# Loading q by single tokens in 256-byte rows, and spacing the attention work of a block's two groups

## The chip, the cores and the metric

The kernel runs on one core of a Trainium2 chip. The metric is the device time of one execution in microseconds (us), lower is better. A core has a matrix engine (TensorE, PE in the profile; its weight loads are listed as PEld), a vector engine (VectorE, DVE), a scalar engine (ScalarE, ACT), a general engine (GpSimd, POOL) and a sync engine (SyncE, SP) that only issues DMAs here. They run side by side and wait for each other by semaphores. 16 DMA engines move data between the chip's memory (HBM) and the on-chip SBUF; TensorE writes its sums to PSUM.

## The reference

Attention in chunks of 64 tokens, then a feed-forward network with a squared ReLU:

```python
B, H, S, D = (8, 8, 576, 64)               # q, k, v, float32
q_c = q.reshape(B, H, 9, 64, D)            # k_c, v_c likewise
scores = 1 / sqrt(D) * q_c @ k_c^T
attn = exp(scores - max) / sum             # along a row of 64
out = attn @ v_c
x = out.transpose(0, 2, 1, 3).reshape(B * S, H * D)     # 4608 x 512
result = max(x @ w_in, 0) ** 2 @ w_out     # w_in 512 x 2048, w_out 2048 x 512
```

## The kernel before

**Tiling.** The 4608 tokens are cut into 18 groups of 256 (a sequence of 576 tokens ends inside some groups), and two groups make a block of the feed-forward network: 9 blocks (the second one takes groups 3 and 2). While block j goes through the network, the groups of block j + 1 go through attention, and q, k and v of block j + 2 are loaded.

**One group's attention** is a chain of steps, each a function:

- `qk_pieces` and `v_pieces` yield the loads, each a DMA that SP issues. Groups 0 to 3 load q and k by pairs of tokens. From group 4 on (`FIRST_DMA_T`), q is loaded by pairs of tokens, in rows of 512 bytes (L103), and k by single tokens, in rows of 256 bytes (L111), a DMA for each 128 tokens or part of them. q and k have five buffers.
- `cast_qk` (C in the plan) makes bfloat16 copies `qkb` of q (L218) and k (L221): on GpSimd for groups 4 to 7, on ScalarE from group 8.
- `transpose_qk_dma` (TD) has one DMA transpose both into `qkT` (L227), issued by SP. The groups before 4 are transposed by TensorE instead (L165).
- `scores` (SC) runs 32 matmuls of 64 x 64 x 64 (L249) into one PSUM tile `ps_att`, of which there are two, and ScalarE takes the exponential (L256). As q lies in pairs, the queries of 64 tokens are two runs of 32 columns, read alternately: the helper `queries` gives this view, in which neighbouring columns are 1,024 bytes apart.
- `values` (AV) runs 64 matmuls in two halves (L273), each half into a `ps_att` tile, and VectorE divides by the row sum (L280, L281).
- `transpose_x` (XT) transposes the result into `xT`: on TensorE with a copy for groups 2 to 5 (L300, L305), with a DMA that SP issues from group 6 on (L294).

**The feed-forward work** is a generator that yields after each unit; a unit is a *slot*. `ffn_in` has a slot for each of 16 column tiles of `w_in` (32 in block 1, which works in halves of 256 tokens): four matmuls (L336), the ReLU on ScalarE (L347) and the square on VectorE (L351) or ScalarE (L349). `ffn_out` computes a 2 x 2 product with seven quarter products instead of eight, in 14 slots of eight matmuls each (L404), with copies on ScalarE (L439, L448, L475), sums on VectorE (L364) and stores of the output that GpSimd issues (L423). Block 0 uses a plain second layer (L485).

**The order of the work** is written out by hand. After each slot, the loop issues one piece of the pending loads, if the slot is in `go_slots`, and then the steps that `plan` has for that slot. Each engine and SP's queue run their instructions in this order. So a transpose on SP stands behind all loads of earlier slots, and scores on TensorE stand in front of all feed-forward matmuls of later slots. The slot tables are at L557 to L592: in block 2, for instance, scores of the next block's groups are at slots 8 and 11, values at 12 and 14, xT at 15 and 17.

Of the kernel before, what the change touches and what calls it, by code (L numbers as in the profile page):

```python
# [17 lines left out]
def kernel(  # L18
# [9 lines left out]
    nc = tc.nc  # L28

    B, H, S, D = q.shape  # L30
# [7 lines left out]
    GT = 256  # L38
# [3 lines left out]
    FIRST_DMA_T = 4  # L42
# [33 lines left out]
    def segments(g0, n):  # L76
        while n:
            b, s = divmod(g0, S)
            m = min(n, S - s)
            yield b, s, m  # L80
            g0 += m
            n -= m

    qk = {}

    def runs(g):

        for t in range(GT // 128):
            p = 0
            for b, s, m in segments(g * GT + t * 128, 128):  # L90
                yield t, p, m, b, s
                p += m

    def qk_pieces(g):
        q_sb = in_pool.tile([128, 2, H, D], FP32, name="q_sb")
        k_sb = in_pool.tile([128, 2, H, D], FP32, name="k_sb")
        qk[g] = (q_sb, k_sb)

        pairs = ((q_sb, q), (k_sb, k)) if g < FIRST_DMA_T else ((q_sb, q),)
        p = 0  # L100
        for b, s, m in segments(g * GT, GT):
            for dst, src in pairs:
                yield lambda dst=dst, src=src, b=b, s=s, p=p, m=m: nc.sync.dma_start(  # L103
                    out=dst.rearrange("p t h d -> p (t h d)")[p:p + m // 2, :].rearrange(
                        "p (h e) -> p h e", h=H),
                    in_=src[b, :, s:s + m, :].rearrange("h (s i) d -> s h (i d)", i=2))
            p += m // 2
        if g < FIRST_DMA_T:
            return
        for t, p, m, b, s in runs(g):  # L110
            yield lambda b=b, s=s, t=t, p=p, m=m: nc.sync.dma_start(  # L111
                out=k_sb[p:p + m, t, :, :],
                in_=k[b, :, s:s + m, :].rearrange("h s d -> s h d"))

    def v_pieces(g):

# [96 lines left out]
    def cast_qk(g):  # L213
        qkb = att_pool.tile([128, 2, 2 * H * D], BF16, name="qkb", bufs=2)
        state["qkb", g] = qkb
        copy = nc.gpsimd.tensor_copy if g < 8 else nc.scalar.copy
        q_sb, k_sb = (x.rearrange("p t h d -> p (t h d)") for x in qk[g])
        copy(  # L218
            out=qkb[:, 0].rearrange("p (i h d) -> p i h d", i=2, h=H),
            in_=q_sb.rearrange("p (h i d) -> p i h d", h=H, i=2))  # L220
        copy(out=qkb[:, 1], in_=k_sb)  # L221

    def transpose_qk_dma(g):
        qkb = state.pop(("qkb", g))
# [5 lines left out]

    def scores(g):
        qkT = state.pop(("qkT", g))

        def queries(a, t, hp, p):
            x = qkT[64 * a:64 * a + 64, 0]
            if g < FIRST_DMA_T:
                return x[:, t, hp, p * 64:p * 64 + 64]
            p0 = (2 * t + p) * 32
            return x[:, :, hp, p0:p0 + 32].rearrange("c i p -> c p i")

        ps = ps_att.tile([128, 1024], FP32, name="ps_att")
        for hp in range(n_hp):
            for t in range(2):
                for a in range(2):
                    for p in range(2):
                        c = p ^ a
                        cols = slice(p * 64, p * 64 + 64)
                        o0 = a * 512 + hp * 128 + t * 64
                        nc.tensor.matmul(  # L249
                            out=ps[64 * c:64 * c + 64, o0:o0 + 64],  # L250
                            lhsT=qkT[64 * a:64 * a + 64, 1, t, hp, cols],
                            rhs=queries(a, t, hp, p),
                            start=True, stop=True)
        e = att_pool.tile([128, 2, n_hp, 2, 64], BF16, name="e")
        state["e", g] = e
        nc.scalar.activation(  # L256
            out=e.rearrange("p a h t q -> p (a h t q)"), in_=ps, func=AF.Exp, scale=scale)
# [48 lines left out]

    C, TD = cast_qk, transpose_qk_dma
    SC, AV, XT = scores, values, transpose_x

    def TA(g):  # L310
# [55 lines left out]
    def sum_quarters(out, in0, in1, op=ALU.add, half=slice(None)):  # L366
        return lambda _: add(nc.vector, out[:, half], in0[:, half], in1[:, half], op)
# [110 lines left out]
    def ffn_out_by_ft(j):  # L478

        gT = gTs.pop(j)  # L480
        n_tt = len(blocks[j]) * GT // 128
        o_ps = [ps_ffn.tile([128, d_model], FP32, name="ps_ffn") for _ in range(n_tt)]

        def mm(tt, ft):
            nc.tensor.matmul(  # L485
                out=o_ps[tt],
                lhsT=gT[:, ft, tt * 128:(tt + 1) * 128],
                rhs=w_out_bf[:, ft, :],
                start=(ft == 0), stop=(ft == n_ft - 1))

        for ft in range(n_ft - 4):
            for tt in range(n_tt):
                mm(tt, ft)
            yield
        for tt in range(n_tt):
            for ft in range(n_ft - 4, n_ft):
                mm(tt, ft)
            o_sb = ffn_pool.tile([128, d_model], FP32, name="o_sb", bufs=4)
            nc.scalar.copy(out=o_sb, in_=o_ps[tt])
            t0 = blocks[j][tt // 2] * GT + tt % 2 * 128  # L500
            nc.gpsimd.dma_start(out=out[t0:t0 + 128, :], in_=o_sb)
# [44 lines left out]
    for j, grps in enumerate(blocks):  # L546
        nxt = blocks[j + 1] if j + 1 < len(blocks) else []
        far = blocks[j + 2] if j + 2 < len(blocks) else []
        plan = {}

        def at(slot, f, g):
            plan.setdefault(slot, []).append((f, g))

        if j == 0:
            loads, go_slots = pieces(far), range(17)
            at(28, sum_quarters(b11_p_b21, b11, b21), None)
            for slot, f in ((24, TA), (27, SC), (29, AV), (31, XT)):  # L557
                at(slot, f, nxt[0])
            at(31, TQ, nxt[1])
            at(31, sum_quarters(b11_m_b22, b11, b22, ALU.subtract), None)  # L560
            phases = [ffn_in(0, [(0, 512, range(n_ft))]), ffn_out_by_ft(0)]
        elif j == 1:
            loads, go_slots = itertools.chain(*map(qk_pieces, far)), range(26, 48)
            for slot, f in ((1, TK), (4, SC), (7, AV), (11, XT)):
                at(slot, f, grps[1])
            for i, g in enumerate(nxt):
                for slot, f in ((16 + 4 * i, C), (21 + 4 * i, TD), (37 + i, SC), (39 + 2 * i, AV),
                                (42 + 2 * i, XT)):
                    at(slot, f, g)
            for i, g in enumerate(far):  # L570
                at(36 + 4 * i, C, g)
                at(42 + 3 * i, TD, g)
            at(2, sum_quarters(b11_p_b12, b11, b12), None)
            at(12, sum_quarters(b12_p_b22, b12, b22), None)
            at(20, sum_quarters(b21_p_b22, b21, b22), None)
            phases = [ffn_in(1, [(0, 256, FT_ORDER), (256, 256, FT_ORDER)]), ffn_out(1)]
        else:
            loads, go_slots = pieces(far), range(32)
            slots = {SC: (4, 4), AV: (7, 10), XT: (11, 13), C: (18, 22), TD: (20, 24)}
            if j == 3:  # L580
                slots.update({SC: (6, 6), AV: (9, 11), XT: (12, 14)})
            if j == 2:
                loads = itertools.chain(*map(v_pieces, nxt), loads)
                slots = {SC: (8, 11), AV: (12, 14), XT: (15, 17), C: (20, 23), TD: (22, 25)}
                go_slots = [*range(18), *range(26, 32)]
            for f in (SC, AV, XT):
                for i, g in enumerate(nxt):
                    at(slots[f][i], f, g)
            for f in (C, TD):
                for i, g in enumerate(far):  # L590
                    at(slots[f][i], f, g)
            phases = [ffn_in(j, [(0, BT, FT_ORDER)]), ffn_out(j)]  # L592
        slot = 0
# [41 lines left out]
```

## Time and profile before

| | |
|---|---|
| median of 7 runs | 291.61 us (290.22 to 296.98) |
| profiled execution | 290.98 us, of it the span from first to last instruction 289.2 us |
| TensorE busy | 274.3 us |
| VectorE, ScalarE, GpSimd busy | 188.3, 161.6, 53.2 us |
| DMA packets | 141,648, of them 110,448 under 512 bytes; 57.09 MB |
| score matmuls (L249) | 576, busy 11.2 us |
| loads of q in 512 KB | 12, median 6.9 us from issue to landing |
| loads of k in 256 KB | 25, median 6.3 us from issue to landing |
| transposes of q and k | 14, median 5.4 us from issue to landing |

The profile is of one execution. Busy time is the time in which an engine has work in it; time in which it stands is put down to what ended it (`[1.01 <-DMA ...]` is a stand of 1.01 us that a DMA ended). The chain of waits goes back from the last instruction: at each step to what released it, or to the instruction before it on its engine. A line such as `L249` is a line of the kernel before. The DMA share is the mean over the 16 DMA engines of the time that their packets took; transfers overlap, so in short stretches it can pass 100%.

### The profile page before, as it was taken

The numbers are of one execution on the slowest core, as the hardware profiler recorded it, in microseconds if no ns is written. First come the engines' busy times: TensorE is split into PE (matmuls) and PEld (weight loads), VectorE is DVE, ScalarE is ACT, GpSimd is POOL, SyncE is SP. The second block draws the span as 40 slices with busy tenths as digits, with TensorE's granted clock in tenths as the row PEclk, the third lists the DMA queues.
The fourth block names the chain that finished last, engine by engine and source line by source line (L and its number), as shares of the span: only waits on it lengthen the run. The fifth ranks groups of instructions, "written<-read, shape, count | busy, mean of one in ns | idle before, by whom it ended". The sixth has DMA issues, their size and how long they took to land.

```text
span 289.2 us, 7266 instructions
## 1 busy us (share of the span) xinstructions
PE 274.3 (95%) x3014; PEld 182.5 (63%) x3014; DVE 188.3 (65%) x305; ACT 161.6 (56%) x270; POOL 53.2 (18%) x85
## 2 busy tenths in 40 slices
PE   2999999989999999989989999999999999999994
PEld 1774455778874488547844785478548844884583
DVE  1256414889854496479637973797389648965793
ACT  1527605776348753866376738763876387308710
POOL 2037744051161003000200021002000200030012
PEclk9999999999999999999999999999999999999999
DMA  7999999999999999998999999978994931121003
GB/s 199 240 332 358 365 320 213 292 222 202 218 181 271 238 194 252 268 224 167 200 257 218 176 198 300 200 134 187 309 214 86 169 124 36 39 99 48 2 18 127
DMA packets 141648, 57.09 MB, mean 197 GB/s; under 512 B 110448, under 2 KB 137328, under 8 KB 141616
## 3 DMA queue, kind: packets, MB, share of 16 engines
q1 hardware_dynamic: 138640, 47.33, 78.6%
q0 software_dynamic: 2832, 9.18, 8.7%
q8 instruction: 23, 0.38, 0.6%
q10 hardware_dynamic: 144, 0.13, 0.1%
q14 instruction: 9, 0.07, 0.1%
HBM read 36.70 MB, written 9.44 MB: 160 GB/s over the span
## 4 chain that ended last, share of the span: by engine, by line
PE 84%; DVE 5%; DMA 5%; ACT 3%; issue 1%; SPq 0%; ACTq 0%
PE ps_ffn L336 37%; PE ps_ffn L404 33%; PE ps_ffn L485 5%; DMA qkT<-qkb 3%; PE ps_att L249 3%; PE ps_att L273 2%; DVE gT L351 2%; ACT rl L347 2%; DMA k_sb<-in_k_dram 2%; PE ps_ffn L211 2%; DVE x L281 2%; PE ps_ffn L165 1%; PE ps_att L300 1%; PE ps_ffn L200 0%; DVE w_out_bf L364 0%
## 5 line engine op out<-in xcount | busy, mean ns | idle before, releaser
L336 PE MATMUL ps_ffn<-xT,w_in_bf 128*128 128x512 bf16 (+1 forms) x640 | 130.1, 358 | 1.1 <-ACT rl L347 0.6
L351 DVE TENSOR_TENSOR gT<-rl 128x512 bf16<-128x512 f32 (+2 forms) x132 | 75.4, 596 | 64.4 <-ACT rl L347 62.9
L347 ACT ACTIVATE rl<-ps_ffn 128x512 f32<-128x512 f32 (+2 forms) x160 | 85.3, 553 | 34.1 <-PE ps_ffn L336 31.5
L336 PEld LDWEIGHTS <-w_in_bf 128*128 128x128 bf16 x640 | 60.6, 98 | 58.7 <-issue 1.3
L404 PEld LDWEIGHTS <-w_st 128*128 128x128 bf16 x640 | 62.3, 98 | 7.6
L423 POOL DMA_DIRECT2D out_dram<-o_sb x29 | 20.8, 717 | 157.7 <-DVE o_sb L364 152.2
L364 DVE TENSOR_TENSOR w_st<-gT 128x2048 bf16<-128x2048 bf16 x40 | 47.4, 1219 | 0.2
L404 PE MATMUL ps_ffn<-w_out_bf,w_st 128*128 128x256 bf16 x384 | 45.0, 273 | 0.0
L404 PE MATMUL ps_ffn<-w_sum,w_st 128*128 128x256 bf16 x256 | 29.6, 273 | 0.0
L404 PEld LDWEIGHTS <-gT 128*128 128x128 bf16 x256 | 25.1, 98 | 4.4
L281 DVE TENSOR_TENSOR x<-ps_att,rec 128x512 bf16<-128x512 f32 x36 | 24.9, 692 | 1.2
L475 ACT COPY o_sb<-ps_ffn 128x512 f32<-128x512 f32 (+1 forms) x8 | 4.5, 560 | 34.7 <-PE ps_ffn L404 34.7
L256 ACT ACTIVATE e<-ps_att 128x1024 bf16<-128x1024 f32 x18 | 17.9, 1020 | 7.7 <-PE ps_att L249 7.5
L349 ACT ACTIVATE gT<-rl 128x512 bf16<-128x512 f32 (+2 forms) x28 | 16.8, 600 | 0.9
L404 PE MATMUL ps_ffn<-w_out_bf,gT 128*128 128x256 bf16 x128 | 15.3, 273 | 0.0
L404 PE MATMUL ps_ffn<-w_sum,gT 128*128 128x256 bf16 x128 | 15.3, 272 | 0.0
L485 PE MATMUL ps_ffn<-w_out_bf,gT 128*128 128x512 bf16 x64 | 14.7, 379 | 0.3 <-ACT rl L347 0.3
L273 PEld LDWEIGHTS <-e 64*64 64x64 bf16 x576 | 7.0, 107 | 9.4 <-DVE x L281 2.7
L249 PEld LDWEIGHTS <-qkT 64*64 64x64 bf16 x576 | 8.8, 109 | 6.2 <-issue 4.0
L249 PE MATMUL ps_att<-qkT 64*64 64x64 bf16 x576 | 11.2, 219 | 1.4 <-DMA qkT<-qkb 1.0
L140 POOL CAST w_in_bf<-w_st 128x1024 bf16<-128x1024 f32 (+1 forms) x9 | 9.0, 1004 | 18.7 <-DMA w_st<-in_moe_w_in_dram 18.6
L273 PE MATMUL ps_att<-ve_sb,e 64*64 64x65 bf16 x288 | 9.9, 197 | 1.9 <-DVE x L281 1.1
(51 smaller groups left out, 161.6 us busy)
## 6 DMA issues: line engine op xcount, KB each, us to landing
out_dram<-o_sb POOLq DMA_DIRECT2D x33, 256.0 KB, 4.7
k_sb<-in_k_dram SPq DMA_DIRECT2D x25, 256.0 KB, 6.3
q_sb<-in_q_dram SPq DMA_DIRECT2D x12, 512.0 KB, 6.9
ve_sb<-in_v_dram SPq DMA_DIRECT2D x32, 128.0 KB, 4.4
vo_sb<-in_v_dram SPq DMA_DIRECT2D x32, 128.0 KB, 3.9
w_st<-in_moe_w_in_dram SPq DMA_DIRECT2D x8, 512.0 KB, 6.7
w_st<-in_moe_w_out_dram SPq DMA_DIRECT2D x8, 512.0 KB, 6.3
k_sb<-in_k_dram SPq DMA_DIRECT2D x3, 512.0 KB, 7.2
```

The lines of the kernel that those rows point to most:

```text
L249: nc.tensor.matmul(out=ps[64 * c:64 * c + 64, o0:o0 + 64], lhsT=qkT[64 * a:64 * a + 64, 1, t, hp, cols], rhs=queries(a, t, hp, p), start=T ...
L256: nc.scalar.activation(out=e.rearrange("p a h t q -> p (a h t q)"), in_=ps, func=AF.Exp, scale=scale)
L273: nc.tensor.matmul(out=ps[64 * p:64 * p + 64, a, hp * (D + 1):(hp + 1) * (D + 1)], lhsT=e[64 * c:64 * c + 64, a, hp, t, :], rhs=vb[64 * c: ...
L281: nc.vector.tensor_tensor(out=x[:, t].rearrange("p h a d -> p a h d"), in0=o[:, :, :, 0:D], in1=rec.to_broadcast([128, 2, n_hp, D]), op=AL ...
L336: nc.tensor.matmul(out=h[:, 0:n], lhsT=w_in_bf[:, dt, ft * 128:(ft + 1) * 128], rhs=xT[:, c // 128:(c + n) // 128, dt, :], start=(dt == 0) ...
L347: nc.scalar.activation(out=rl[:, 0:n], in_=h[:, 0:n], func=AF.Relu)
L349: nc.scalar.activation(out=gT[:, ft, c:c + n], in_=rl[:, 0:n], func=AF.Square)
L351: nc.vector.tensor_tensor(out=gT[:, ft, c:c + n], in0=rl[:, 0:n], in1=rl[:, 0:n], op=ALU.mult)
L364: engine.tensor_tensor(out=out, in0=in0, in1=in1, op=op)
L404: nc.tensor.matmul(out=outs[t], lhsT=a[:, i, t * 128:(t + 1) * 128], rhs=b[:, i, :], start=(first and i == 0 and (last or t == 0)), stop=( ...
L423: dma.dma_start(out=out[t0:t0 + HT, col:col + HD].rearrange("(t p) d -> p t d", p=128), in_=o_sb.rearrange("p (t d) -> p t d", d=HD))
L485: nc.tensor.matmul(out=o_ps[tt], lhsT=gT[:, ft, tt * 128:(tt + 1) * 128], rhs=w_out_bf[:, ft, :], start=(ft == 0), stop=(ft == n_ft - 1))
```

## The change

From group 4 on, q is loaded as k is: by single tokens, in rows of 256 bytes, one DMA for each 128 tokens or part of them, q and k in turn. The cast of q no longer reorders, and the scores read 64 neighbouring columns of `qkT` for every group. SP issues 160 instructions instead of 135.

In the plan, block 1 has scores, values and xT of groups 4 and 5 one slot earlier, and xT of its own second group one slot later. In block 2 the second scores go from slot 11 to 10, the second values from 14 to 15 and the second xT from 17 to 18; in block 3 the second values from 11 to 12 and the second xT from 14 to 15. In the blocks after, scores go from slot 4 to 5, values from 7 and 10 to 8 and 11, the second xT from 13 to 14. Since loads are issued one a slot, and there are two or three more a block, loads of v come later in SP's order, in block 2 partly behind the transposes of q and k.

```diff
     def qk_pieces(g):
...
-        pairs = ((q_sb, q), (k_sb, k)) if g < FIRST_DMA_T else ((q_sb, q),)
...
         for t, p, m, b, s in runs(g):
-            yield lambda b=b, s=s, t=t, p=p, m=m: nc.sync.dma_start(
-                out=k_sb[p:p + m, t, :, :],
-                in_=k[b, :, s:s + m, :].rearrange("h s d -> s h d"))
+            for dst, src in ((q_sb, q), (k_sb, k)):
+                yield lambda dst=dst, src=src, b=b, s=s, t=t, p=p, m=m: nc.sync.dma_start(
+                    out=dst[p:p + m, t, :, :],
+                    in_=src[b, :, s:s + m, :].rearrange("h s d -> s h d"))
...
     def cast_qk(g):
-        copy = nc.gpsimd.tensor_copy if g < 8 else nc.scalar.copy
-        q_sb, k_sb = (x.rearrange("p t h d -> p (t h d)") for x in qk[g])
-        copy(
-            out=qkb[:, 0].rearrange("p (i h d) -> p i h d", i=2, h=H),
-            in_=q_sb.rearrange("p (h i d) -> p i h d", h=H, i=2))
-        copy(out=qkb[:, 1], in_=k_sb)
+        for which in range(2):
+            copy = nc.gpsimd.tensor_copy if g < 8 else nc.scalar.copy
+            copy(out=qkb[:, which], in_=qk[g][which].rearrange("p t h d -> p (t h d)"))
...
     def scores(g):
-        def queries(a, t, hp, p):
-            x = qkT[64 * a:64 * a + 64, 0]
-            if g < FIRST_DMA_T:
-                return x[:, t, hp, p * 64:p * 64 + 64]
-            p0 = (2 * t + p) * 32
-            return x[:, :, hp, p0:p0 + 32].rearrange("c i p -> c p i")
...
-                            rhs=queries(a, t, hp, p),
+                            rhs=qkT[64 * a:64 * a + 64, 0, t, hp, p * 64:p * 64 + 64],
...
-            for slot, f in ((1, TK), (4, SC), (7, AV), (11, XT)):
+            for slot, f in ((1, TK), (4, SC), (7, AV), (12, XT)):
...
-                for slot, f in ((16 + 4 * i, C), (21 + 4 * i, TD), (37 + i, SC), (39 + 2 * i, AV),
-                                (42 + 2 * i, XT)):
+                for slot, f in ((16 + 4 * i, C), (21 + 4 * i, TD), (36 + i, SC), (38 + 2 * i, AV),
+                                (41 + 2 * i, XT)):
...
-            slots = {SC: (4, 4), AV: (7, 10), XT: (11, 13), C: (18, 22), TD: (20, 24)}
+            slots = {SC: (5, 5), AV: (8, 11), XT: (11, 14), C: (18, 22), TD: (20, 24)}
             if j == 3:
-                slots.update({SC: (6, 6), AV: (9, 11), XT: (12, 14)})
+                slots.update({SC: (6, 6), AV: (9, 12), XT: (12, 15)})
             if j == 2:
-                slots = {SC: (8, 11), AV: (12, 14), XT: (15, 17), C: (20, 23), TD: (22, 25)}
+                slots = {SC: (8, 10), AV: (12, 15), XT: (15, 18), C: (20, 23), TD: (22, 25)}
```

More of the change, by code (lines that the diff above doesn't have):

```diff
@@ L97, in qk_pieces @@
         qk[g] = (q_sb, k_sb)
-        pairs = ((q_sb, q), (k_sb, k)) if g < FIRST_DMA_T else ((q_sb, q),)
[L100 to L107, printed above, removed]
-        if g < FIRST_DMA_T:
+        if g < FIRST_DMA_T:
+            p = 0
+            for b, s, m in segments(g * GT, GT):
+                for dst, src in ((q_sb, q), (k_sb, k)):
+                    yield lambda dst=dst, src=src, b=b, s=s, p=p, m=m: nc.sync.dma_start(
+                        out=dst.rearrange("p t h d -> p (t h d)")[p:p + m // 2, :].rearrange(
+                            "p (h e) -> p h e", h=H),
+                        in_=src[b, :, s:s + m, :].rearrange("h (s i) d -> s h (i d)", i=2))
+                p += m // 2
             return
         for t, p, m, b, s in runs(g):
-            yield lambda b=b, s=s, t=t, p=p, m=m: nc.sync.dma_start(
-                out=k_sb[p:p + m, t, :, :],
-                in_=k[b, :, s:s + m, :].rearrange("h s d -> s h d"))
+            for dst, src in ((q_sb, q), (k_sb, k)):
+                yield lambda dst=dst, src=src, b=b, s=s, t=t, p=p, m=m: nc.sync.dma_start(
+                    out=dst[p:p + m, t, :, :],
+                    in_=src[b, :, s:s + m, :].rearrange("h s d -> s h d"))
     def v_pieces(g):
```

## The prediction

> **What bounds the kernel now.** I read the page's first two parts, then the chain in order of time, then TensorE's timeline around each place where the chain leaves TensorE, then the DMA queue's.
>
> ```profile
> PE 274.3 (95%) x3014; PEld 182.5 (63%) x3014; DVE 188.3 (65%) x305; ACT 161.6 (56%) x270; POOL 53.2 (18%) x85
> ...
> DMA  7999999999999999998999999978994931121003
> ```
>
> TensorE is busy for 95% of the span, so it is the bound. But the DMA engines are full as well, in nearly every slice up to number 27 (about 200 us). Two limits lie close together, and the change takes from one and adds to the other.
>
> The chain in order of time (start, length, what):
>
> ```profile
> 45.58 0.38 PE ps_att L249 x32
> ...
> 74.20 0.62 PE ps_att L249 x32
> ...
> 120.75 1.11 PE ps_att L249 x64
> ...
> 140.90 9.14 DMA qkT<-qkb
> 150.05 0.04 issue
> 150.09 0.69 PE ps_att L249 x32
> ```
>
> 32 score matmuls of a group with contiguous queries (groups 0 to 3; the first row is group 3) take 0.38 us. A group with strided queries takes 0.62 alone and 1.11 for a pair. And once, at 150.05, the chain leaves TensorE for a DMA: the transpose of q and k of group 11, issued at 140.90. All of TensorE's waits for this cause and for the spacing of the values stand in its timeline:
>
> ```profile
> 98.56 0.22 PE L273 MATMUL ps_att<-ve_sb,e 64*64 64x65 bf16 x2 [0.42 <-ACT e L256]
> ...
> 101.19 0.22 PE L273 MATMUL ps_att<-ve_sb,e 64*64 64x65 bf16 x2 [0.21 <-DVE x L281]
> ...
> 127.19 0.22 PE L273 MATMUL ps_att<-ve_sb,e 64*64 64x65 bf16 x2 [0.40 <-DVE x L281]
> ...
> 128.03 0.22 PE L273 MATMUL ps_att<-ve_sb,e 64*64 64x65 bf16 x2 [0.51 <-DVE x L281]
> ...
> 150.09 0.69 PE L249 MATMUL ps_att<-qkT 64*64 64x64 bf16 x32 [1.01 <-DMA qkT<-qkb]
> ```
>
> From 150.05 to 247 the windows view gives TensorE 96.73 us busy of 96.95: after that wait it is never short of work.
>
> **The change part by part** (sums against the profiled execution: span 289.2, time 290.98, of which 1.8 lies around the span; the median of 291.61 is 0.2% above it).
>
> *Contiguous score reads.* 14 groups (4 to 17) fall from 0.62 to 0.38 alone (0.24) or from 1.11 to 0.76 a pair (0.35). Groups 4 to 7 stand alone, the rest in pairs: 4 x 0.24 + 5 x 0.35 = 2.7 us, all of it TensorE's own time. Of it 1.3 (groups 4 to 9) lies before the wait at 150, 1.4 after.
>
> *Slots.* Values of block 2's next groups go from slots 12 and 14 to 12 and 15 with the second scores a slot earlier: the waits of 0.42 and 0.21 go, 0.6. In block 3 they go from 9 and 11 to 9 and 12: 0.40 + 0.51 falls to what blocks with three slots already show (under 0.2), so 0.7. Groups 4 and 5 one slot up bring xT of group 5 earlier: at 85.06 TensorE stood 0.23 for that copy, 0.2. From block 4 on, scores go from slot 4 to 5, which is no work but one unit (0.87 us: five units of first-layer matmuls in 4.32) more in front of scores that may be late. Without any late DMA TensorE would end 2.7 + 0.6 + 0.7 + 0.2 + 1.0 (the wait at 150) = 5.2 us earlier: 285.8.
>
> *q in 256-byte rows.* Per group 1,024 packets of 512 bytes become 2,048 of 256. Packet costs come from two short stretches of the DMA view, of 512-byte rows (150 to 151 us) and of 256-byte rows (94 to 97 us):
>
> ```profile
> q1 hardware_dynamic: 660, 0.34, 115.8%
> ```
>
> ```profile
> q1 hardware_dynamic: 2684, 0.67, 107.0%
> ```
>
> Share x 16 engines x length / packets: 28.1 ns and 19.1 ns. Two small for one large cost 10.1 ns more, x 64 packets an engine = 0.65 us a group. Landings say less: issue time plus time to landing puts 512 KB of q 1.8 us behind its predecessor (groups 8 and 9), and 512 KB of k, which is in 256-byte rows already, 1.7 and 2.3: a difference of -0.1 to 0.5. I take 0.25 a group, nearer to the landings since a queue that is full is seen in those, and keep 0.1 and 0.65 as ends.
>
> Here a rule speaks against the change. The Trainium skill, "DMA: Bandwidth & Descriptors", Specifications, asks for 512 bytes for line rate and says that less is read, modified and written; were a byte then twice as dear, q of a group would take 3.7 instead of 1.85 us, 8 groups 14.8 us, and the time would be about 302. The k rows do not bear that out: 256-byte rows of k land about as fast as q's. The same page's "Why small descriptors are slow" gives 3 cycles a packet, 22 for 19, so an estimate of 0.3 a group; the row's side stays.
>
> *SP's queue.* 25 more DMA instructions, two or three a block, at least 0.45 us each. SP's issues last up to 4.2 us because the queue behind is full, so they cost nothing while it is; with that cover gone, 2 x 0.45 = 0.9 a block, more than 2 x 0.25. Values and transposes of the same block stand behind them. In block 2 both transposes move ahead of two loads of values (good for them by 1 us), while the last piece of k of group 9 goes behind an xT transpose; ScalarE's cast of it can then stand up to 3 us, but the next ScalarE work behind it has idle time in front:
>
> ```profile
> 114.75 0.59 ACT L475 COPY o_sb<-ps_ffn 128x512 f32<-128x512 f32 x1 [4.51 <-PE ps_ffn L404]
> ```
>
> The casts themselves stay (1.05 us for q and for k in the lines view).
>
> *Where the DMAs come late.* The stream has no slack up to block 3's transposes: SP reaches group 10's at 138.87, when its cast has been done since 136.18 (135.13 + 1.05), and group 11's at 140.90, 1.2 us after its cast. Loads of eight groups (4 to 11) lie before it, so 8 x 0.25 = 2.0 us late. Of the 9.1 us that group 11's took, part is chance: from 142 to 147 the DMA view shows 125 GB/s, with one 16 KB instruction packet and almost nothing moving in the last microsecond and a half. The same transfer in other blocks took 3.9 to 7.5. I credit 0.9, half of that hole: landing at 150.05 + 2.0 - 0.9 = 151.15.
>
> *Sum.* TensorE arrives early: 1.3 + 0.6 + 0.7 + 0.2 = 2.8 us ahead, 149.08 + 0.87 - 0.24 - 2.8 = 146.9, and waits 4.2 us. So the gains before that point are spent, and the time follows from the landing: group 11's scores start at 151.2 instead of 150.09 (+1.1), have one more unit behind them (-0.87), are shorter (-0.24), and three pairs follow (-1.05): -1.05. 290.98 - 1.05 = 289.9. Earlier transposes have room: group 9's landed at 118.6 for 121.3. Later ones too: block 4's landed 3.7 us ahead of their scores, later ones 2.4 to 3.3, and a slot is added.
>
> A second rule bears on that wait: "TensorE: Matmul & The Clock Gate" (the HAM clock gate) says that an idle window of about 3.4 us halves TensorE's clock until it has been busy as long. The waits of before, 1.01 at most after the start, cost only themselves. At the start, after 5 us without work, eight identity matmuls took 1.03 us (at 7.76) and later 0.62 (at 11.41), while the clock row shows full speed. By the waits of before the sum stays 289.9; by the rule 1.7 us more, 291.6, if the free-running window falls wholly inside 4.2 us, which is about one time in four. I leave it to the range.
>
> **The rivals.**
> 1. *The DMAs keep up* (0.2). For it: after about 132 us many DMA slots are not full and values land within 2.6 us of issue, so the stream could absorb q's packets there. Against: it was late by 1.01 already. If group 11's lands before 149, the time is 285.8 to 288; 287 stands for it.
> 2. *The DMA stream becomes the bound* (0.3): slower. Place: group 11's scores. Price: by packet times 8 x 0.65 = 5.2 us, landing at 155.2 without the credit, so 5.1 - 0.87 - 0.24 - 1.05 = +2.9: 293.9; at 0.45 a group +1.3: 292.3. It decides from a landing at 152.25 on, 2.2 us later than before, or 0.28 us a group without the credit. That is close to my value, hence the weight.
> 3. *The reads are not faster* (under 0.05): the 0.62 could be due to the full DMA rather than the stride. Against: those of groups 3 and 2 took 0.38 and 0.37 in equally full slices. Then 289.9 + 1.3 = 291.2.
>
> **How the numbers follow.** The likeliest case (0.5) is 289.9, itself 288.3 to 291. What a measurement of this kernel can tell from no change is about 0.3%, 0.9 us: faster means under 290.1 on the profiled execution's scale. Faster: all of rival 1 and six tenths of the likeliest, 0.5. Same: most of the rest of it and a sixth of rival 2, 0.24. Slower: 0.26. The range goes from 286.5 (most of rival 1) to 293.4 (rival 2 short of its upper bound, or the clock's 1.7 on top of the likeliest).
>
> **What would show it.** Right: 32 score matmuls at 0.38 in every group; 1.0 us less waiting for values in blocks 2 and 3; about 4 us of TensorE waiting for the transposed q and k in block 4, and none after; q packets of 256 bytes at k's cost. Wrong: no wait at block 4 (then near 286), waits for it in blocks 2 or 3 or in each block from 5 on (then the stream's period exceeds TensorE's and the loss grows by block), slow matmuls after the wait, or casts on ScalarE that hold up its PSUM copies.

## The result and the profile after

The change is slower. Its executions have a median of 294.0 us (292.32 to 299.44, 14 of them), those of the kernel before, on the same chips, 291.45 us (289.48 to 299.45, 35 of them). The ratio is 1.0098, with a 95% interval of 1.0074 to 1.0123. Executions of one kernel scatter by several us here, so a ratio is taken between those that lie within 1.5% of each kernel's fastest, and is not the quotient of the medians. The forecast was 289.9 in a range of 286.5 to 293.4.

The profiled execution of the change took 292.41 us, with a span of 290.6: 1.4 us more than the profiled execution before. The page's busy times and DMA rows:

```profile
PE 271.9 (94%) x3014; PEld 180.3 (62%) x3014; DVE 188.8 (65%) x305; ACT 161.7 (56%) x270; POOL 55.4 (19%) x85
...
DMA  8999999999999899999999999898997921121003
...
DMA packets 156177, 57.10 MB, mean 196 GB/s; under 512 B 139312, under 2 KB 151856, under 8 KB 156144
```

TensorE has 2.4 us less work than before (274.3 to 271.9), and the span is longer: it stands more. The chain in order of time (start, length, what) says where:

```profile
109.19 5.86 DMA xT<-x
115.05 0.04 issue
115.09 6.23 PE ps_ffn L325 x28
...
140.37 5.12 DMA xT<-x
145.49 0.04 issue
145.53 2.62 PE ps_ffn L325 x12
148.15 4.51 DMA qkT<-qkb
152.66 0.04 issue
152.70 0.44 PE ps_att L238 x32
```

Before, the chain left TensorE for one late transpose, at 150.05. Now it does so three times: for the second half of `xT` at the starts of blocks 3 and 4, and for `qkT` of group 11. (L325 is the first layer, L336 before; L238 the scores, L249 before; L262 the values; L283 and L224 SP's transposes into `xT` and `qkT`.) TensorE's timeline gives the length of each stand:

```profile
75.53 0.45 PE L238 MATMUL ps_att<-qkT 64*64 64x64 bf16 x32 [0.48 <-DMA qkT<-qkb]
...
115.09 1.25 PE L325 MATMUL ps_ffn<-xT,w_in_bf 128*128 128x512 bf16 x5 [1.74 <-DMA xT<-x]
...
145.53 5.34 PE L325 MATMUL ps_ffn<-xT,w_in_bf 128*128 128x512 bf16 x24 [1.70 <-DMA xT<-x]
150.90 0.45 PE L238 MATMUL ps_att<-qkT 64*64 64x64 bf16 x32
152.70 0.44 PE L238 MATMUL ps_att<-qkT 64*64 64x64 bf16 x32 [1.36 <-DMA qkT<-qkb]
```

The scores themselves are as forecast. In this view 32 of them take 0.44 to 0.45 us, as those of groups 2 and 3 did before the change, where a group with strided queries took 0.69; a pair falls from 1.18 to 0.71 to 0.73. But what they saved is spent. The first matmul of each phase, and the end, in the two profiled executions:

| us | before | change | change minus before |
|---|---|---|---|
| second layer of block 1 | 68.8 | 69.17 | +0.4 |
| block 2 | 85.06 | 85.04 | 0.0 |
| its second layer | 102.32 | 100.91 | -1.4 |
| block 3 | 114.55 | 115.09 | +0.5 |
| its second layer | 131.75 | 131.44 | -0.3 |
| block 4 | 143.98 | 145.53 | +1.6 |
| its second layer | 161.44 | 162.72 | +1.3 |
| block 5 | 173.67 | 174.94 | +1.3 |
| block 8 | 259.14 | 260.51 | +1.4 |
| end | 289.2 | 290.6 | +1.4 |

Blocks 2 and 3 gain 1.4 and 0.8 us while they compute, and with the two waits for `xT` the start of the block that follows moves back by 1.9 each time. After block 4 nothing changes any more, neither way, though each block's scores are shorter. That leaves two questions: why the transposes are late, and why the later blocks gain nothing.

SP's queue before block 4 shows the first. Here it is in the kernel before (start, length on SP, what):

```profile
133.42 1.28 SPq L294 DMA_TRANSPOSE xT<-x  x1
134.74 1.26 SPq L118 DMA_DIRECT2D ve_sb<-in_v_dram  x2
136.11 1.27 SPq L294 DMA_TRANSPOSE xT<-x  x1
137.42 1.35 SPq L125 DMA_DIRECT2D vo_sb<-in_v_dram  x2
138.87 6.24 SPq L227 DMA_TRANSPOSE qkT<-qkb  x2
```

And in the change:

```profile
136.65 1.66 SPq L283 DMA_TRANSPOSE xT<-x  x1
138.36 0.58 SPq L125 DMA_DIRECT2D vo_sb<-in_v_dram  x1
139.00 1.27 SPq L118 DMA_DIRECT2D ve_sb<-in_v_dram  x2
140.37 1.44 SPq L283 DMA_TRANSPOSE xT<-x  x1
141.85 0.58 SPq L118 DMA_DIRECT2D ve_sb<-in_v_dram  x1
142.48 2.20 SPq L125 DMA_DIRECT2D vo_sb<-in_v_dram  x2
144.78 5.90 SPq L224 DMA_TRANSPOSE qkT<-qkb  x2
```

The first `xT` goes out 3.2 us later, the second 4.3, and the pair for `qkT` 5.9: six loads of v instead of four lie between the first transpose and the last, each a block ahead of its use. The casts are not the cause: ScalarE ended that of group 11 at 139.36, 139.67 before.

The later blocks are shown by ScalarE and VectorE around the scores of block 5. ScalarE in the change:

```profile
180.38 0.60 ACT L336 ACTIVATE rl<-ps_ffn 128x512 f32<-128x512 f32 x1 [0.33 <-PE ps_ffn L325]
180.88 1.94 ACT L245 ACTIVATE e<-ps_att 128x1024 bf16<-128x1024 f32 x2
182.69 0.62 ACT L336 ACTIVATE rl<-ps_ffn 128x512 f32<-128x512 f32 x1
183.34 0.63 ACT L338 ACTIVATE gT<-rl 128x512 bf16<-128x512 f32 x1
```

VectorE after it:

```profile
184.49 1.29 DVE L340 TENSOR_TENSOR gT<-rl 128x512 bf16<-128x512 f32 x2 [2.78 <-ACT rl L336]
185.70 0.20 DVE L269 RECIPROCAL rec<-ps_att 128x8 f32<-128x8 f32 x1
185.93 0.69 DVE L270 TENSOR_TENSOR x<-ps_att,rec 128x512 bf16<-128x512 f32 x1
186.54 0.20 DVE L269 RECIPROCAL rec<-ps_att 128x8 f32<-128x8 f32 x1
186.77 0.69 DVE L270 TENSOR_TENSOR x<-ps_att,rec 128x512 bf16<-128x512 f32 x1
```

The two exponentials hold ScalarE for 1.94 us; a ReLU and a square done by ScalarE itself stand behind them, so VectorE gets no ReLU to square for 2.78 us, and the two divisions of the first group's values stand behind those squares, though TensorE had ended these values by 184.0. TensorE's next values need a free `ps_att` tile and wait for the second division, which ends at 187.46:

```profile
187.52 0.22 PE L262 MATMUL ps_att<-ve_sb,e 64*64 64x65 bf16 x2 [0.51 <-DVE x L270]
```

Before, TensorE stood for 0.05 us at this place. A block takes 28.53 us (block 5 to 6), 28.49 before: what the scores save in TensorE is waited for.

### The profile page after: what moved, and what is told of

The parts are those of the page before. It is cut to its first block, busy times and chain, and to the rows that moved or that the text cites. A ratio compares the mean times of both kernels' runs of the same rounds, so it can differ in the third digit from the quotient of the medians.

```text
span 290.6 us, 7284 instructions
## 1 busy us (share of the span) xinstructions
PE 271.9 (94%) x3014; PEld 180.3 (62%) x3014; DVE 188.8 (65%) x305; ACT 161.7 (56%) x270; POOL 55.4 (19%) x85
## 3 DMA queue, kind: packets, MB, share of 16 engines
q1 hardware_dynamic: 153168, 47.33, 77.2%
## 4 chain that ended last, share of the span: by engine, by line
PE 45%; DVE 6%; DMA 5%; ACT 4%; issue 2%; ACTq 0%
PE ps_ffn L393 23%; PE ps_ffn L325 21%; DMA xT<-x 4%; ACT rl L336 2%; DVE x L270 2%; DVE gT L340 2%; ACT e L245 2%; DMA qkT<-qkb 2%; DVE w_st L353 1%; PE ps_att L262 1%; DVE o_sb L353 0%; DVE rec L269 0%; PE ps_att L238 0%; DVE o_sb L464 0%; ACT gT L338 0%
## 5 line engine op out<-in xcount | busy, mean ns | idle before, releaser
L325 PE MATMUL ps_ffn<-xT,w_in_bf 128*128 128x512 bf16 (+1 forms) x640 | 129.9, 358 | 3.7 <-DMA xT<-x 3.4
L336 ACT ACTIVATE rl<-ps_ffn 128x512 f32<-128x512 f32 (+2 forms) x160 | 85.6, 553 | 33.8 <-PE ps_ffn L325 30.9
L325 PEld LDWEIGHTS <-w_in_bf 128*128 128x128 bf16 x640 | 60.5, 98 | 61.4 <-issue 2.1
L262 PEld LDWEIGHTS <-e 64*64 64x64 bf16 x576 | 6.9, 107 | 9.5 <-DVE x L270 4.6
L218 ACT CAST qkb<-q_sb 128x1024 bf16<-128x1024 f32 x10 | 10.5, 1048 | 2.4 <-DMA q_sb<-in_q_dram 2.4
L262 PE MATMUL ps_att<-ve_sb,e 64*64 64x65 bf16 x288 | 9.5, 197 | 2.2 <-DVE x L270 2.1
L218 ACT CAST qkb<-k_sb 128x1024 bf16<-128x1024 f32 x10 | 10.5, 1046 | 1.5 <-DMA k_sb<-in_k_dram 1.5
```

The lines of the kernel that those rows point to most:

```text
L218: copy(out=qkb[:, which], in_=qk[g][which].rearrange("p t h d -> p (t h d)"))
L262: nc.tensor.matmul(out=ps[64 * p:64 * p + 64, a, hp * (D + 1):(hp + 1) * (D + 1)], lhsT=e[64 * c:64 * c + 64, a, hp, t, :], rhs=vb[64 * c: ...
L325: nc.tensor.matmul(out=h[:, 0:n], lhsT=w_in_bf[:, dt, ft * 128:(ft + 1) * 128], rhs=xT[:, c // 128:(c + n) // 128, dt, :], start=(dt == 0) ...
L336: nc.scalar.activation(out=rl[:, 0:n], in_=h[:, 0:n], func=AF.Relu)
```

## Experiments

The tables of times give the median of the executions, how many there were, and the ratio to the kernel before on the same chip with its 95% interval.

### The parts alone

**Loads and reads, without the slots.** The change with all slots of the kernel before (those of blocks 1 and 3 too, left out here):

```diff
...
-            slots = {SC: (5, 5), AV: (8, 11), XT: (11, 14), C: (18, 22), TD: (20, 24)}
+            slots = {SC: (4, 4), AV: (7, 10), XT: (11, 13), C: (18, 22), TD: (20, 24)}
...
-                slots = {SC: (8, 10), AV: (12, 15), XT: (15, 18), C: (20, 23), TD: (22, 25)}
+                slots = {SC: (8, 11), AV: (12, 14), XT: (15, 17), C: (20, 23), TD: (22, 25)}
```

> The changed loads, cast and score reads with the slots of before. Theory A (the DMA stream is what costs: the loads of q in twice as many rows and more DMAs come late at blocks 3 and 4): slower than before by 1.5 us or more, 292.5 to 294, with waits for transposed q and k or xT in blocks 2 to 4 of some 4 us. Theory B (the slots are what costs: xT one slot later on SP and scores one slot later on the engines): the score reads' gain shows, 288 to 290.5, and little waiting for DMAs beyond the 1.0 us of before.

**Slots alone.** The loads and reads of the kernel before, with the slots of the change (the same lines the other way round).

> The loads and reads of before with the slots of the change. Theory A: no slower than before, 289.5 to 291: 1.3 us less waiting for values in blocks 2 and 3 and no wait at block 4, against 0.5 us of new waiting for values in each of blocks 5 to 7. Theory B: slower, 292 to 294, with the waits for xT at the starts of blocks 3 and 4 present (1.7 us each).

**Reads alone.** Rows of 512 bytes stay; the scores read two runs of 32 neighbouring columns one after the other, so they come out in another order, and the exponential puts them back:

```diff
-            return x[:, :, hp, p0:p0 + 32].rearrange("c i p -> c p i")
+            return x[:, :, hp, p0:p0 + 32]
...
+            nc.scalar.activation(
+                out=e.rearrange("p a h t (q i) -> p (a h t) i q", i=2),
+                in_=ps.rearrange("p (n i q) -> p n i q", i=2, q=32), func=AF.Exp, scale=scale)
```

> The kernel before, q still in 512-byte rows, but the scores read each 64 queries as two runs of 32 neighbouring columns, and the exponential writes its result back in the order of the tokens. So the score reads alone change, not the DMAs. If strided reads cost 0.24 us a group, 32 score matmuls take 0.38 us in every group here too. Both theories: the gain before the wait in block 4 (1.3 us) goes into that wait, what follows it keeps 1.3: 289.3 to 290. If the strided exponential takes more than its 1.02 us, ScalarE gives some of it back.

| kernel | median us | n | ratio |
|---|---|---|---|
| loads and reads | 295.99 | 6 | 1.0193 (1.0143 to 1.0242) |
| slots | 292.62 | 7 | 1.0077 (1.0047 to 1.0107) |
| reads | 292.62 | 10 | 1.0074 (1.0032 to 1.0117) |
| before beside them | 294.64 (289.89 to 298.22) | 17 | |

No part alone is faster. The loads and reads take longer than either theory said; five of their six executions have a mean clock of 0.988 to 0.994, and half clock shows in the trace. The waits view (engine, work, releaser: sum in us, how often, longest) of the loads and reads has one line for `qkT` that is over three times the 1.0 us of the kernel before:

```profile
PE ps_att L238 <- DMA qkT<-qkb: 3.9, 3, 2.2
```

Two of the three waits, 2.22 and 1.14 us, end at 151.61 and 153.19. What follows them is in the windows view of the same execution (stretch, length, TensorE's busy time and matmuls, granted clock, DMA share, GB/s):

```profile
150.00:153.00 3.00, 0.45 (x32) 1.00 1.09 285
153.00:156.00 3.00, 2.81 (x39) 0.66 1.14 239
156.00:159.00 3.00, 3.00 (x42) 0.77 1.32 222
159.00:162.00 3.00, 3.00 (x45) 1.00 1.26 215
```

For some 3.4 us TensorE runs at half clock: (1 - 0.66) x 3 + (1 - 0.77) x 3 = 1.7 us lost, on top of the waits. That is the rule of the Trainium skill that the prediction left to the range ("TensorE: Matmul & The Clock Gate", the HAM clock gate). Two waits with scores between them were enough for it, and neither was as long as its window.

The slots did what they say to the values: no wait for them over 0.25 us is left. In their place came 1.37 us for `xT` at 115.94 and 1.18 for `qkT` at 151.66. So the moved slots are enough to make transposes late, with no DMA added.

The reads alone say the most about the blocks after. Nothing waits for `qkT` or `xT` there, TensorE's busy time is 271.9 as in the change, and the time is still longer, where 289.3 to 290 was expected. The exponential pays for its order of writing (ScalarE's timeline, block 5):

```profile
179.09 2.46 ACT L260 ACTIVATE e<-ps_att 128x1024 bf16<-128x1024 f32 x2
```

2.46 instead of 1.94 us for two, and the waits for values in a block grow from 0.05 to 0.28 + 0.51 us; the block takes 28.83 us. Half a microsecond more on ScalarE beats 0.35 less on TensorE: in the attention slots of these blocks TensorE waits for ScalarE's and VectorE's chain.

### The later scores

The change with scores, values and `xT` of the blocks from 4 on in the slots of the kernel before:

```diff
-            slots = {SC: (5, 5), AV: (8, 11), XT: (11, 14), C: (18, 22), TD: (20, 24)}
+            slots = {SC: (4, 4), AV: (7, 10), XT: (11, 13), C: (18, 22), TD: (20, 24)}
```

> The change, but in blocks 4 to 7 scores, values and xT stand in their old slots (4; 7 and 10; 11 and 13). If the wait of 0.51 us for values in blocks 5, 6 and 7 is due to scores in slot 5 (their exponentials then meet the ReLU and square that ScalarE has for tile 14), it goes, and the time falls by 1.5 us for it and rises by up to 0.9 at block 4, where the scores wait for the transposed q and k one unit longer: 292.5 to 293.5 with the change at 293 to 294. If the wait is due to late DMAs, it stays and the time does not fall.

295.02 us (6 executions), ratio 1.0138 (1.0109 to 1.0168), longer than the 292.5 to 293.5 expected. The waits for values in blocks 5 to 7 fall from 0.51 to 0.38, and a block takes 28.35 us: 0.14 less than before the change, 0.18 less than the change. But in block 4 the scores come before their transposes twice, by 0.81 and 1.36 us, and half clock follows here too (0.74 from 152 to 156 us, 0.84 from 156 to 160). So slot 5 costs 0.18 us in each block from 5 on; that it is of use in block 4 rests on one execution of each kernel. Even in slot 4 a block gains only 0.14 of the 0.35 us.

### The price of rows and of DMAs

Two kernels from the one before. In the first only q's rows become 256 bytes, from group 4 on; the number of DMAs stays, and so does the order of `qkT`'s columns, so the reads stay slow (the cast has nothing left to reorder, and takes as long):

```diff
...
+                else:
...
+                        out=dst[p:p + m // 2],
+                        in_=src[b, :, s:s + m, :].rearrange("h (s i) d -> s i h d", i=2))
...
-            out=qkb[:, 0].rearrange("p (i h d) -> p i h d", i=2, h=H),
-            in_=q_sb.rearrange("p (h i d) -> p i h d", h=H, i=2))
+            out=qkb[:, 0], in_=q_sb)
```

> The kernel before with as many DMAs, slots and strided score reads as before, but q lands in rows of 256 bytes (a partition's two tokens in two rows). So the packet size alone changes. If the packets are what makes the stream late: the transposes of q and k of group 11 land later by 8 times 0.25 to 0.65 us, and the time rises by 2 to 5 us, to 293 to 296. If the number of DMA instructions is: within 0.5 us of before.

In the second the rows stay at 512 bytes and each of q's DMAs of 128 tokens or more is cut in two, 16 DMAs more, each into half as many partitions:

```diff
+                cuts = [(0, m)] if g < FIRST_DMA_T or m < 128 else [(0, m // 2), (m // 2, m)]
+                for lo, hi in cuts:
...
```

> The kernel before with q still in rows of 512 bytes, but each DMA of q over 128 tokens or more is cut into two: as many DMA instructions as the change has, packets as before. If the number of DMAs is what makes the stream late (0.45 us and more each on SP, two or three a block): later at block 4 by 2 to 4 us, 293 to 295. If the packets are: within 0.5 us of before.

The first took 297.08 us (6 executions, ratio 1.0254, 1.0188 to 1.032), the second 299.37 (6, 1.0331, 1.0242 to 1.0421), the kernel before beside them 295.97 (289.59 to 297.31, 12). Both are above what was expected, and half clock is part of it: four of the first's executions and all six of the second's have a mean clock of 0.987 to 0.994; the first's other two took 295.93 and 297.22. By the ratios each alone costs more than the whole change. Both show the late transposes. The waits view of the first:

```profile
PE ps_att L253 <- DMA qkT<-qkb: 2.4, 2, 1.5
...
PE ps_ffn L340 <- DMA xT<-x: 1.7, 2, 1.2
```

And of the second:

```profile
PE ps_att L251 <- DMA qkT<-qkb: 4.5, 2, 3.6
```

In the second, the clock is 0.74, 0.50 and 0.62 in the three windows of 3 us after 153: 3.4 us lost to it, twice the loss above.

The time in which SP reaches the pair of transposes for `qkT` of block 3 (groups 10 and 11) measures what each does to the stream. Counted from the first matmul of block 2, in the profile of each kernel:

| kernel | SP issues the pair, us after block 2's start |
|---|---|
| before, first profile | 53.8 |
| before, another profile | 53.1 |
| before with the reads alone | 52.8 |
| slots alone | 56.0 |
| rows of 256 bytes alone | 58.7 |
| loads and reads alone | 59.0 |
| q's DMAs cut in two | 59.6 |
| change | 59.7 |

Each row is one profile; the first three, whose slots and loads are the same, lie within 1.0. Against their mean, 53.2, the slots cost 2.8 us, the rows 5.4 and the cut DMAs 6.4. About 0.5 of the rows' 5.4 can be TensorE's own wait at the start of block 3, which moves all later slots. That leaves 4.9 to 5.4 us for eight groups, 0.61 to 0.68 a group on the average. It does not come evenly: 1.3 us are there when block 2's loads of v begin, 1.8 and 1.5 come while SP issues the loads of groups 8 to 11, 2.1 while it issues block 2's two transposes into `qkT`, and 1.3 are won back in between. The costs don't add: the change has the rows, the slots and 12 more DMAs, and comes to 6.5.

### The place of the second `xT`

The change, with the second `xT` of blocks 2 and 3 where it was before:

```diff
-                slots.update({SC: (6, 6), AV: (9, 12), XT: (12, 15)})
+                slots.update({SC: (6, 6), AV: (9, 12), XT: (12, 14)})
...
-                slots = {SC: (8, 10), AV: (12, 15), XT: (15, 18), C: (20, 23), TD: (22, 25)}
+                slots = {SC: (8, 10), AV: (12, 15), XT: (15, 17), C: (20, 23), TD: (22, 25)}
```

> The change with the second xT of blocks 2 and 3 a slot earlier (17 and 14, its values stay at 15 and 12), so that one load fewer stands before it on SP. The waits of 1.74 and 1.70 us for xT at the starts of blocks 3 and 4 fall by 0.5 to 1 each. If these waits are what costs, the time falls by 1 to 2 us; if they only stand in front of the wait for transposed q and k in block 4, which ends when its DMA lands, that wait grows by as much and the time stays within 0.5 us of the change's 293 to 294.

294.55 us (6 executions), ratio 1.0163 (1.0029 to 1.0296): not told apart from the change. The wait in front of block 3 falls to 0.80 us, that of block 4 stays at 1.89, and `qkT` is waited for by 0.47 and 1.39. For block 4 SP's queue sets the transpose, not its slot: the second `xT` of block 3 goes out 55.3 us after block 2's start with either slot, and the pair for `qkT` at 60.5.

The other way round, the kernel before with slots moved only where its own profile showed waits:

```diff
-                slots.update({SC: (6, 6), AV: (9, 11), XT: (12, 14)})
+                slots.update({SC: (6, 6), AV: (9, 12), XT: (12, 14)})
+            if j == 4:
+                slots.update({SC: (7, 7), AV: (10, 13), XT: (13, 15)})
...
-                slots = {SC: (8, 11), AV: (12, 14), XT: (15, 17), C: (20, 23), TD: (22, 25)}
+                slots = {SC: (8, 10), AV: (12, 15), XT: (15, 17), C: (20, 23), TD: (22, 25)}
```

> The kernel before, with slots moved only where its trace shows a wait: values three slots apart in blocks 2 and 3, second scores of block 2 a slot earlier, and in block 4 scores at slot 7, values at 10 and 13, xT at 13 and 15. Loads, casts and reads are those of before. If the waits of before (0.6 and 0.7 us for values, 1.0 for the transposed q and k) go and nothing else comes: 288 to 289, and no half-speed clock after the wait in block 4.

293.67 us (6 executions), ratio 1.0125 (1.0023 to 1.0228): a miss. The waits for values are gone, and 1.84 us for `xT` at 116.66 and 1.66 for `qkT` at 180.50 came. Here the second `xT` is not moved in blocks 2 and 3, only the values in front of it, and SP still reaches the pair at 56.4. So the slots' 2.8 us do not hang on the `xT` slot alone. SP is held up in block 2, where it issues the two transposes into `qkT`. In the kernel before and with the slots alone:

```profile
109.84 5.12 SPq L227 DMA_TRANSPOSE qkT<-qkb  x2
```

```profile
111.47 8.01 SPq L227 DMA_TRANSPOSE qkT<-qkb  x2
```

With these slots it takes 8.3 us, with the rows alone 7.1 and in the change 8.1, though their casts are done in time with the slots (at 110.5 for 111.47). Why a transpose holds SP longer there is open.

### The loads of v behind the transposes

If the transposes are late because they stand behind loads, the loads that nobody waits for can go behind them. From block 3 on, SP issues q and k first, then the transposes, and v afterwards. On the kernel before:

```diff
-            loads, go_slots = pieces(far), range(32)
+            loads, go_slots = pieces(far), [*range(8), *range(25, 30)]
```

> The kernel before, but from block 3 on the loads of v are issued behind the transposes of q and k, not ahead of them (some 8 to 10 loads, 5 us of SP's queue). If the late DMA stream at block 4 is what decides the time and its scatter: the transposes of groups 10 and 11 go out when their casts are done (about 136 and 140) and land by 146, the wait of 1.0 us goes, no half-speed clock follows, and nearly every execution takes 289 to 290.5. If the stream is not the cause: no change, or slower by v coming late to the values.

On the change:

```diff
-            loads, go_slots = pieces(far), range(32)
+            loads, go_slots = pieces(far), [*range(10), *range(25, 30)]
```

> The change with the same reordering of v's loads. If it is the stream that took the change's gain: the wait of 1.4 us for transposed q and k in block 4 goes, and xT for block 4 lands before it starts (1.7 us less), so 290 to 291. The wait for xT at block 3 (1.7) stays, since block 2's order is not touched. If the slots or the reads are what costs, it stays at 293 to 294.

And the kernel before once more, unchanged, for the scatter of its stream:

> The kernel before once more, unchanged, for a second profile of it. If the landing of group 11's transposes at 150.05 was a lucky one, it lands later here, by 1 to 4 us, with a longer wait in block 4; if the trace before was typical, within 0.5 us of it relative to the start of block 4.

| kernel | median us | n | ratio |
|---|---|---|---|
| before, v late | 291.2 (289.78 to 294.77) | 22 | 1.0003 (0.998 to 1.0026) |
| change, v late | 290.71 (287.67 to 296.57) | 22 | 0.9963 (0.9929 to 0.9998) |
| before beside them | 292.17 (289.71 to 298.97) | 43 | |

This order of SP's queue takes the ratio of the change from 1.0098 to 0.9963 and leaves that of the kernel before where it was. What it does to the scatter the ratio does not show: of the kernel before, 20 of 43 executions took over 294 us, and 20 had a mean clock of 0.987 to 0.994. With v late, one of 22 took over 294 us, the one with a mean clock of 0.994. The change with v late has one such execution of 22 too, though 6 with such a clock. So most of the long executions go with the loads of v in front of the transposes, as was expected. None of them was traced. SP's queue of the change with v late, over the same part as above:

```profile
133.74 3.85 SPq L283 DMA_TRANSPOSE xT<-x  x2
137.69 5.58 SPq L224 DMA_TRANSPOSE qkT<-qkb  x2
143.32 1.83 SPq L118 DMA_DIRECT2D ve_sb<-in_v_dram  x2
```

The four transposes go out in a row, the pair for `qkT` 53.2 us after block 2's start, as early as before the change. TensorE waits for neither group (its timeline), though the second transpose, issued at 139.43, landed only at 148.16, while the first group's scores ran:

```profile
142.53 5.34 PE L325 MATMUL ps_ffn<-xT,w_in_bf 128*128 128x512 bf16 x24
147.81 0.84 PE L238 MATMUL ps_att<-qkT 64*64 64x64 bf16 x64
```

Block 4 starts at 142.53 and has no wait for a transpose, where it lost 1.70 + 1.36 us in the change. What is left is 1.16 us for `xT` at the start of block 3, whose transposes are issued in block 2, and 0.42 and 0.44 for `qkT` in block 1; neither block's loads were moved.

The unchanged kernel took 291.3 us, and neither expectation came. Group 11's transpose was not later but earlier: it landed at 148.29 in a block that started at 145.48, against 150.05 and 143.98 in the first profile. Between these two executions it moved by some 3 us against TensorE, so the 1.01 us that the prediction built on was one draw of it.

Last, all that helped together: the change, v late, the second `xT` of blocks 2 and 3 a slot earlier, and the old slots from block 5 on.

```diff
-            loads, go_slots = pieces(far), range(32)
+            loads, go_slots = pieces(far), [*range(10), *range(25, 30)]
...
+            if j > 4:
+                slots.update({SC: (4, 4), AV: (7, 10), XT: (11, 13)})
```

> The change with v's loads behind the transposes from block 3 on (as in the run before), and slots set by what its trace still showed: the second xT of blocks 2 and 3 at 17 and 14, and from block 5 on scores, values and xT back in slots 4, 7 and 10, 11 and 13. If the stream was the cause and the rest is what the trace shows: 0.4 to 0.8 us less waiting for xT at block 3, 0.15 us less in each of blocks 5 to 7, so a profiled span near 286 and a time of 287 to 290, below both kernels. If the wait for xT at block 3 is bound to the stream and not to its slot, within 0.5 us of the run before.

289.37 us (287.79 to 292.92, 19 executions), beside 293.55 for the kernel before (24 executions); ratio 0.9952 (0.9922 to 0.9983). By the ratios it is faster than both kernels. Its waits for transposes in the whole execution, from the waits view:

```profile
PE ps_att L238 <- DMA qkT<-qkb: 0.8, 2, 0.5
...
PE ps_ffn L325 <- DMA xT<-x: 0.7, 1, 0.7
```

The intervals of this kernel and of the change with v late overlap, so what the last two edits add is not shown.

## Why the prediction was wrong

**Its likeliest case failed at two of its steps, and their sizes make up the miss.** It had group 11's `qkT` landing at 151.15 and 1.05 us saved by the three pairs behind it. The transpose landed at 152.66, 1.5 later, and the pairs behind saved nothing: 289.9 + 1.5 + 1.05 = 292.45, and the profiled execution took 292.41.

**The step that failed: the stream, "8 x 0.25 = 2.0 us late".** SP reached the pair 5.9 us later. Two terms were mis-sized. The row price was taken at 0.25 us a group, near the landings; the rows alone cost 0.61 to 0.68. That is the size of the other working, 0.65 from packet times, but not its mechanism: the packets took no longer in all with the rows alone (77.2% of a span of 295.2 us, 78.6% of 289.2 before: 228 and 227 us), so the agreement is luck as far as is known. And the slots were priced on TensorE only; they hold SP up by 2.8 us by themselves. The credit of 0.9 us for chance in the landing was too small rather than too large: group 11's transpose was issued 7.2 us later (148.15 for 140.90), but landed after 4.51 us instead of 9.14, so 2.6 us later than before. The count of added DMAs was wrong as well: the page's list of issues has 24 DMAs of q before and 36 after, 12 more and not 25 (SP's DMAs are 195 and 183 in the traces, where 160 and 135 were given above). That they "cost nothing while" the queue is full did not hold where q's DMAs were cut: 16 more, at the same rows, made SP 6.4 us later.

**The missed step: `xT` stands in the same queue.** The prediction priced one late transpose and wrote that the earlier ones had room. It looked at `qkT` alone. The second `xT` of blocks 2 and 3 was both moved a slot later and pushed back by the loads in front of it, and TensorE needs it with the first matmuls of the next block: it stood for 1.74 and 1.70 us, and before for neither. So the gain was not spent in one wait of 4.2 us but in three, of 1.74, 1.70 and 1.36: 4.8. The gain itself was nearly right: 2.8 us were forecast up to there, and 2.6 came, 0.4 in the second layer of block 1, 1.4 in block 2 and 0.8 in block 3.

**"Slot 4 to 5, which is no work", and three pairs at 0.35.** It is no work for TensorE. But the windows view that showed TensorE full from 150 to 247 us did not show that ScalarE's exponentials and VectorE's divisions end just before TensorE needs them. With less to do, TensorE waits for them: a block goes from 28.49 to 28.53 us. In slot 4 it goes to 28.35, so the step kept 0.14 of the 0.35 forecast, and slot 5 took that away.

**The clock gate, "about one time in four".** The rule was the right one to name, and its 1.7 us is what the windows view measures. The chance was too low: it asked for one idle stretch as long as the window, where two waits of 0.81 and 1.36 us were enough in one kernel. Of the 15 executions of the change whose clock is recorded, 8 have a mean of 0.980 to 0.994 (one piece of 3.4 us at half clock takes 0.006 off), and they are nearly all of the longer ones; the profiled one has 0.998. This fits the 1.6 us between the profiled execution and the median, though which waits set it off in those executions no trace shows. But half clock is not new with the change: beside the experiments the kernel before has such a mean in 49 of 96 executions, so that its waits "cost only themselves" holds for its two profiled executions and not for every other. The other rule, of 512 bytes, had the direction right and the size not: it gave 14.8 us for eight groups, SP lost 5.4 with the rows alone, and q in 256-byte rows lands as k does (5.3 and 5.0 us from issue, median).

**What was right.** The scores take what those of groups 2 and 3 take, 2.4 us less on TensorE of the 2.7 forecast. The values' waits in block 2 are gone; in block 3 one of 0.51 us is left. The rival that came true is the second, the DMA stream as the bound: its place was right, its turning point at a landing of 152.25 was passed, and its price at "0.45 a group", 292.3, is close to the profiled execution, by luck, since it came by way of waits that it did not name. No cast held the path up, though ScalarE stood 2.4 and 1.5 us in front of casts for q and k.

**What is open.** How the 6.5 us of the change divide between rows, DMAs and slots, as they do not add; by what the rows make SP late, when their packets take no longer in all; and why cutting q's DMAs in two is dearer than the whole change. Each half also fills half as many partitions, which the DMAs of the change do not, and no run tells the number from the shape.

## What to carry to other kernels

Where one queue carries both bulk loads and the transposes that the next block needs first, price an edit by when the queue reaches each of those transposes, not by bytes and not by the matrix engine's work; and put loads that are a block early behind them before adding anything to the queue. A TensorE that never stands can still have another chain right behind it: before counting a saving there, look how long before its use each input was ready. When two ways of costing the same rows differ and the queue is already late, do not settle on the cheaper one.

## What the hardware showed that was not expected

- A wait can cost twice. Waits of 2.22 and 1.14 us, and of 0.81 and 1.36 us, with a few scores between, were each followed by about 3.4 us at half clock (1.7 us more); the change's own waits of 1.70 and 1.36, with 5.8 us between them, were not in its profiled execution (clock 1.00 from 150 to 165).
- Cutting 512 KB loads into halves, with the same bytes and rows, into half as many partitions each, delayed SP by 6.4 us over eight groups; halving the rows delayed it by 5.4.
- Half-sized rows did not raise the total time of the packets: the DMA queue's share is 78.6% of a span of 289.2 us before and 77.2% of 290.6 after, 227 and 224 us, with 14,528 packets more. The stream was later all the same.
- The order of SP's queue bears on how often TensorE's clock falls: in 20 of 43 executions of the kernel before, in 1 of 22 with the loads of v behind the transposes.
- Two exponentials of 128 x 1024 that write bfloat16 into every second element take 2.46 us instead of 1.94.
